# Start of a fused attention and feed-forward kernel: second k projection without filler before it, two normalizations in a row, other places for transposes and loads, last P V copied by two engines

## Chip, cores and metric

One core of one Trainium2 chip. The metric is the device time of one execution in microseconds (us), lower is better. The granted clock is 1.00 unless said otherwise. The kernel before takes 568.5 to 568.9 us (median of the runs beside each experiment); single executions range from 568.42 to 569.41.

## The reference

```python
# attention, batch 8, heads 8, seq 1024, head_dim 64; E and F (64 x 1024) shorten the sequence to 64
k_proj = einsum('ks,bhsd->bhkd', E, k);  v_proj = einsum('ks,bhsd->bhkd', F, v)
attn = softmax(q @ k_proj.T / sqrt(64));  attn_out = attn @ v_proj
# then a gated feed-forward block on 8192 tokens, d_model 512, d_ff 1536
g = x @ w_gate;  out = (g * sigmoid(g) * (x @ w_val)) @ w_out
```

## The kernel before

The program is a hand-made order of units. 16 chunks of 512 tokens (two per batch) go through the feed-forward block; TensorE's products of one chunk are mixed with the attention of later ones. Only the start, where batch 0 has to be worked through before the first product can run, is touched here. Names used below:

- `load_*`: DMAs issued from GpSimd, casting f32 to bf16. `load_w_gv(c0, c1, which)` loads columns 128*c0 to 128*c1 of the gate (0) and/or value (1) weights; block n is column range n, used by product f = n.
- `u_KV` k projection, `u_T` transposes of q, `u_S` scores and exp, `u_R` row sums and reciprocals (VectorE), `u_N` normalization (GpSimd), `u_A` transposes of the normalized scores, `u_PV*` times V and copy to xT.
- `turn` turns E or F by TensorE; `warm(n)` issues n matmuls on zeros whose result nobody reads.
- `put(s, ...)` puts a unit in slot s: slot 2t follows the gate product of step t, slot 2t+1 its value product.

```python
        u_S(0, 0, "g"); u_R(0, 0); u_N(0, 0)
        load_w_gv(1, 2, (1,))
        load_w_gv(2, 3)
        u_T(0, 2, "a", act)
        warm(2)
        u_KV(0, "k", (4, 8), at="y")
        turn(1, "a", (0,), dve)
        # ... KT0, T of u = 1 and 3, second turn of F: unchanged
        u_S(0, 2, "g"); u_R(0, 2); u_N(0, 2)
        load_w_gv(3, 5, (0,))
        u_S(0, 1, "g"); u_R(0, 1); u_N(0, 1)
        u_S(0, 3, "v"); u_R(0, 3); u_N(0, 3)
        load_w_gv(3, 5, (1,))
        # ... A of u = 0, 2; V projections; P V of the first token half
        f_mm(0, 0, 0, 0)
        u_A(0, 1, dve)
        f_mm(0, 0, 1, 0)
        u_PV2(0, 0, 0, 1, dve)
        u_A(0, 3, act)
        f_mm(0, 1, 0, 0)
        u_PV2(0, 0, 1, 1, act)
        f_mm(0, 1, 1, 0)
        # ...
        for i, u in enumerate(range(4, 8)):
            put(11 + i, u_T, 0, u)
```

(Calls on one line, and cuts, are marked by semicolons and "...".)

The softmax here doesn't subtract the row's maximum and nothing guards it: scores larger than these inputs give would overflow.

Of the kernel before, what the change touches and what calls it, by code (L numbers as in the profile page):

```python
# [34 lines left out]
def kernel(  # L35
# [68 lines left out]
    def load_q(b, ch, js=(0, 4), hs=(0, H)):  # L104
        if js[0] == 0 and hs[0] == 0:
            qb[b, ch] = q_pool.tile([P, H, 4, D], BF16, name="qb", tag="qb")
        js, hs = slice(*js), slice(*hs)
        nc.gpsimd.dma_start(  # L108
            out=qb[b, ch][:, hs, js, :].rearrange("p h j d -> p h (j d)"),
            in_=q[b, hs].rearrange("h (p c j) d -> p c h j d", c=2, j=4)[:, ch, :, js, :].rearrange(  # L110
                "p h j d -> p h (j d)"
            ),
        )

    def load_w_gv(c0, c1, which=(0, 1)):
        cs = slice(c0 * P, c1 * P)
        for wsrc, wdst in [((moe_w_gate, wg), (moe_w_val, wv))[i] for i in which]:
            nc.gpsimd.dma_start(
                out=wdst[:, :, cs],
                in_=wsrc[:, cs].rearrange("(t p) c -> p t c", p=P),  # L120
            )
# [11 lines left out]
    def bank(where, shape, dt, name):  # L133
        pool, tag = banks[where]
        return pool.tile(shape, dt, name=name, tag=tag)

    def copy(eng, out, in_):
        (nc.scalar.copy if eng is nc.scalar else eng.tensor_copy)(out=out, in_=in_)  # L138
# [107 lines left out]
    def u_T(b, u, at="a", eng=nc.scalar):  # L246
        ch, w = divmod(u, 4)
        g, i = divmod(w, 2)
        ps = bank(at, [P, 4, P], BF16, "qTp")
        src = qb[b, ch]  # L250
        for n in range(4):
            nc.tensor.transpose(  # L252
                out=ps[:, n, :],
                in_=src[:, 4 * g + n, 2 * i : 2 * i + 2, :].rearrange("p j d -> p (j d)"),
                identity=ident_bf[:],
            )
        t = aw.tile([P, 4, P], BF16, name="qT", tag="qT", bufs=4)
        copy(eng, t[:], ps[:])
        qT[b, u] = t
# [17 lines left out]
    def u_S(b, u, at="a"):  # L277
        ch, w = divmod(u, 4)
        g, i = divmod(w, 2)
        ps = bank(at, [P, 4, P], FP32, "sc")  # L280
        if (b, ch) in BY_DMA:
            t = qT[b, ch, "d"][:].rearrange("p (h i) t -> p i h t", i=2)[:, i, 4 * g : 4 * g + 4]
        else:
            t = qT.pop((b, u))
        for n in range(4):
            nc.tensor.matmul(  # L286
                out=ps[:, n, :], lhsT=t[:, n, :], rhs=BD[b % 2][:, 4 * g + n, :], start=True, stop=True
            )
        e = aw.tile([P, 4, 2, KP], FP32, name="ee", tag="ee", bufs=4)
        nc.scalar.activation(  # L290
            out=e[:].rearrange("p h j k -> p (h j k)"),
            in_=ps[:].rearrange("p a k -> p (a k)"),
            func=AF.Exp,
            scale=scale,
        )
        ee[b, u] = e

    def u_R(b, u):
        e = ee[b, u]
        z = aw.tile([P, 4, 2], FP32, name="zz", tag="zz", bufs=3)  # L300
        nc.vector.reduce_sum(out=z[:], in_=e[:], axis=AX.X)  # L301
        r = aw.tile([P, 4, 2], FP32, name="rr", tag="rr", bufs=4)
        nc.vector.reciprocal(out=r[:], in_=z[:])  # L303
        rr[b, u] = r

    def u_N(b, u, eng=nc.gpsimd):
        ch, w = divmod(u, 4)
        g, i = divmod(w, 2)
        if (b, ch) in BY_DMA:
            if (b, ch, "d") not in AA:  # L310
                AA[b, ch, "d"] = aw.tile([P, 4, H, KP], BF16, name="AAd", tag="AAd")
            a = AA[b, ch, "d"][:, 2 * i : 2 * i + 2, 4 * g : 4 * g + 4, :]
        else:
            a = AA[b, u] = aw.tile([P, 2, 4, KP], BF16, name="AA", tag="AA", bufs=4)
            a = a[:]
        eng.tensor_tensor(  # L316
            out=a.rearrange("p j h k -> p h j k"),
            in0=ee.pop((b, u))[:],
            in1=rr.pop((b, u))[:].unsqueeze(3).to_broadcast([P, 4, 2, KP]),
            op=ALU.mult,  # L320
        )

    def u_A(b, u, eng=nc.vector):
        ch, w = divmod(u, 4)
        g, i = divmod(w, 2)
        if (b, ch) not in AT:
            AT[b, ch] = aw.tile([P, 4, NPAIR, P], BF16, name="AT", tag="AT")
        ps = ps_a.tile([P, 2, 2, P], BF16, name="aTp", tag="pa")
        a = AA.pop((b, u))
        for pr in range(2):  # L330
            for j in range(2):
                nc.tensor.transpose(  # L332
                    out=ps[:, j, pr, :],
                    in_=a[:, j, 2 * pr : 2 * pr + 2, :].rearrange("p h k -> p (h k)"),
                    identity=ident_bf[:],
                )
        copy(eng, AT[b, ch][:, 2 * i : 2 * i + 2, 2 * g : 2 * g + 2, :], ps[:])
# [14 lines left out]
    def u_PV2(b, ch, g, i, eng):  # L352

        if (b, ch) not in xT:
            xT[b, ch] = x_pool.tile([P, NPAIR, CW], BF16, name="xT", tag=f"xT{ch}")
        ps = ps_a.tile([P, 2, CW // 2], FP32, name="pv", tag="pa")
        for n in range(2):
            nc.tensor.matmul(  # L358
                out=ps[:, n].rearrange("p (j t) -> p j t", t=P),
                lhsT=BDV[b % 2][:, 2 * g + n, :],  # L360
                rhs=AT[b, ch][:, 2 * i : 2 * i + 2, 2 * g + n, :],
                start=True,
                stop=True,
            )
        copy(eng, xT[b, ch][:, 2 * g : 2 * g + 2, 256 * i : 256 * (i + 1)], ps[:])

    def u_PV1(b, ch, pr, i, eng):

        ps = ps_a.tile([P, CW // 2], FP32, name="pv", tag="pa")
        nc.tensor.matmul(  # L370
            out=ps[:].rearrange("p (j t) -> p j t", t=P),
            lhsT=BDV[b % 2][:, pr, :],
            rhs=AT[b, ch][:, 2 * i : 2 * i + 2, pr, :],
            start=True,
            stop=True,
        )
        copy(eng, xT[b, ch][:, pr, 256 * i : 256 * (i + 1)], ps[:])
# [82 lines left out]
    def put(s, fn, *a):  # L460
        slots[s].append((fn, a))
# [34 lines left out]
    with tc.manual_schedule():  # L496
# [31 lines left out]
        def warm(n):  # L528

            ps = bank("v", [P, CW], FP32, "warm")  # L530
            for _ in range(n):
                nc.tensor.matmul(  # L532
                    out=ps[:], lhsT=zeros[:, 0:P], rhs=zeros[:],
                    start=True, stop=True,
                )


        dve, act = nc.vector, nc.scalar
# [20 lines left out]
        u_R(0, 0)  # L559
        u_N(0, 0)  # L560
        load_w_gv(1, 2, (1,))
        load_w_gv(2, 3)
        u_T(0, 2, "a", act)
        warm(2)
        u_KV(0, "k", (4, 8), at="y")
        turn(1, "a", (0,), dve)
        u_KT0((2, 4), "vg", (dve, dve, act, act))
# [3 lines left out]
        u_S(0, 2, "g")  # L571
        u_R(0, 2)
        u_N(0, 2)
        load_w_gv(3, 5, (0,))
        u_S(0, 1, "g")
        u_R(0, 1)
        u_N(0, 1)
        u_S(0, 3, "v")
        u_R(0, 3)
        u_N(0, 3)  # L580
        load_w_gv(3, 5, (1,))
        u_A(0, 0, act)
        u_V0w(0, 2, "y")
        u_V0(2, 3, "v")
# [1 line left out]
        u_A(0, 2, dve)  # L586
        u_V0(3, 4, "y")
        u_PV1(0, 0, 2, 0, dve)
        u_PV1(0, 0, 3, 0, act)
        f_mm(0, 0, 0, 0)  # L590
        u_A(0, 1, dve)
        f_mm(0, 0, 1, 0)
        u_PV2(0, 0, 0, 1, dve)
        u_A(0, 3, act)
        f_mm(0, 1, 0, 0)
        u_PV2(0, 0, 1, 1, act)
        f_mm(0, 1, 1, 0)
        nc.vector.memset(ks[1][64:P], 0.0)
        nc.vector.memset(BD[1][:], 0.0)
        nc.vector.memset(BDV[1][:], 0.0)  # L600
        load_w_gv(5, 7)
        load_q(0, 1, hs=(0, 4))
        load_q(0, 1, hs=(4, 8))
        load_w_gv(7, 9)
        load_w_gv(9, 11)
        load_w_gv(11, 12)
        load_q(1, 0)
        load_k(1)
        load_wo(0)
        load_wo(1)  # L610

        for i, u in enumerate(range(4, 8)):
            put(11 + i, u_T, 0, u)
            put(13 + i, u_S, 0, u)
            put(14 + i, u_R, 0, u)
            put(14 + i, u_N, 0, u)
            put((17, 18, 20, 21)[i], u_A, 0, u, nc.scalar)
# [26 lines left out]
        for t in range(NIT):  # L644
            c, f = divmod(t, NFT)
            i = 1 if t < 2 else None
# [39 lines left out]
```

## Time and profile before

| | kernel before |
|---|---|
| time, median of 3 | 568.7 us (568.54 to 569.03) |
| span of the profiled execution | 566.8 us |
| TensorE idle, 10 to 30 us | 1.6 us |
| TensorE idle, 30 to 50 us | 0.1 us |

The span is the time between the first and the last instruction. TensorE is busy for 99% of it, so only what makes TensorE start or stop earlier counts.

Two quantities are used all through. The **landing** of a load is its issue time plus its time to landing. The **lead** of a kernel at some instruction is how much earlier it starts there than the kernel before; I matched TensorE's weight loads of two traces from the end backwards, since the order is the same after the start.

### The profile page before, as it was taken

To read this page: it belongs to the slowest core of one execution; us is meant where nothing else is said; L and a number is where in the kernel's file an instruction comes from. 1 tells how busy PE (TensorE), PEld (TensorE's weight loads), DVE (VectorE), ACT (ScalarE), POOL (GpSimd) and SP (SyncE) were. 2 spreads that over 40 slices of the span, in tenths; PEclk is the share of its full clock that TensorE was granted. 3 is DMA by queue.
4 is the path that set the end of the run, shared out by engine and by line. 5 is a ranking of instruction groups with operands and counts; after the bars stand their busy time and mean duration, and the time that the engine had idled before them with its cause. 6 is when DMAs were issued, how large, how long until landed. Compare 5 with 4: busy or idle time off the path is not lost.

```text
span 566.8 us, 7925 instructions
## 1 busy us (share of the span) xinstructions
PE 560.3 (99%) x2960; PEld 266.2 (47%) x2960; DVE 339.2 (60%) x578; ACT 235.7 (42%) x416; POOL 113.0 (20%) x127
## 2 busy tenths in 40 slices
PE   8999999999999999999999999999999999999997
PEld 4654444444444444444444444444444444444444
DVE  3786664766476645766466655666547665545550
ACT  3564352444435443443434434354343543443222
POOL 6951250123012400123002230023100220000000
PEclk9999999999999999999999999999999999999999
DMA  9999979729913795029930399105990214100012
GB/s 206 191 198 189 176 130 201 134 57 189 194 46 74 117 199 113 38 57 168 189 72 37 77 184 205 38 20 104 196 183 19 58 37 75 38 37 31 26 39 93
DMA packets 112215, 62.78 MB, mean 111 GB/s; under 512 B 66352, under 2 KB 103472, under 8 KB 112176
## 3 DMA queue, kind: packets, MB, share of 16 engines
q0 software_dynamic: 43952, 29.49, 36.5%
q1 hardware_dynamic: 67392, 31.46, 25.6%
q10 hardware_dynamic: 832, 1.31, 0.7%
q8 instruction: 23, 0.38, 0.3%
q14 instruction: 16, 0.13, 0.1%
HBM read 60.29 MB, written 16.78 MB: 136 GB/s over the span
## 4 chain that ended last, share of the span: by engine, by line
PE 97%; ACT 1%; DMA 1%; DVE 0%; issue 0%; POOL 0%
PE yps L433 29%; PE vps L395 29%; PE gps L395 29%; PE kvp L150 3%; PE sc L286 2%; PE pv L343 2%; DMA Eraw<-in_E_dram 1%; ACT ee L290 0%; PE qTp L252 0%; PE aTp L332 0%; PE warm L532 0%; PE efp L520 0%; PE pv L358 0%; ACT AT L138 0%; POOL AA L316 0%
## 5 line engine op out<-in xcount | busy, mean ns | idle before, releaser
L414 DVE SCALAR_TENSOR_TENSOR s<-th,gps 128x512 f32<-128x512 f32 x191 | 129.7, 679 | 134.6 <-ACT th L407 134.3
L395 PE MATMUL vps<-xT,wv 128*128 128x512 bf16 (+1 forms) x776 | 197.5, 377 | 0.0
L395 PE MATMUL gps<-xT,wg 128*128 128x512 bf16 (+1 forms) x772 | 196.9, 377 | 0.0
L433 PE MATMUL yps<-wo,hT 128*128 128x512 bf16 (+1 forms) x780 | 194.5, 376 | 0.0
L407 ACT ACTIVATE th<-gps 128x512 f32<-128x512 f32 x191 | 114.0, 597 | 158.2 <-PE gps L395 151.8
L419 DVE TENSOR_TENSOR hT<-s,vps 128x512 bf16<-128x512 f32 x192 | 131.9, 687 | 20.8 <-DVE s L414 0.5
L316 POOL TENSOR_TENSOR AAd<-ee,rr 128x512 bf16<-128x512 f32 x56 | 58.4, 1042 | 342.0 <-issue 221.9
L433 PEld LDWEIGHTS <-hT 128*128 128x128 bf16 x780 | 76.1, 98 | 89.9
L395 PEld LDWEIGHTS <-wv 128*128 128x128 bf16 x776 | 73.9, 98 | 83.5 <-issue 3.2
L395 PEld LDWEIGHTS <-wg 128*128 128x128 bf16 x776 | 74.0, 98 | 80.9 <-issue 0.8
L443 ACT ACTIVATE ysb<-yps 128x512 f32<-128x512 f32 (+1 forms) x65 | 38.4, 591 | 77.7 <-PE yps L433 77.7
L138 ACT CAST xT<-pv 128x512 bf16<-128x512 f32 (+1 forms) x62 | 35.9, 582 | 51.3 <-PE pv L343 50.3
L301 DVE TENSOR_REDUCE zz<-ee 128x8 f32<-128x512 f32 x64 | 43.5, 679 | 21.9 <-ACT ee L290 21.9
L290 ACT ACTIVATE ee<-sc 128x512 f32<-128x512 f32 x64 | 37.9, 595 | 19.4 <-PE sc L286 18.2
L286 PEld LDWEIGHTS <-qTd 128*128 128x128 bf16 x224 | 17.2, 98 | 13.2
L343 PE MATMUL pv<-AT,BDV 128*128 128x512 bf16 x60 | 22.4, 379 | 0.0
L286 PE MATMUL sc<-BD,qTd 128*128 128x128 bf16 x224 | 21.6, 219 | 0.0
L303 DVE RECIPROCAL rr<-zz 128x8 f32<-128x8 f32 x64 | 13.0, 203 | 6.8 <-DVE zz L301 0.5
L108 POOL DMA_DIRECT2D qb<-in_q_dram x18 | 16.3, 906 | 1.4 <-POOLq L670 0.8
L150 PE MATMUL kvp<-kb,ET 128*64 128x512 bf16 (+1 forms) x72 | 15.5, 358 | 0.0
L162 DVE CAST BDV<-kvp 64x256 bf16<-64x256 f32 x7 | 3.0, 426 | 20.0 <-ACT ks L158 17.8
L150 PE MATMUL kvp<-vb,FT 128*64 128x512 bf16 x56 | 13.4, 382 | 0.0
(73 smaller groups left out, 140.8 us busy)
## 6 DMA issues: line engine op xcount, KB each, us to landing
out_dram<-ysb SPq DMA_DIRECT2D x63, 256.0 KB, 2.3
qb<-in_q_dram POOLq DMA_DIRECT2D x14, 512.0 KB, 17.7
kb<-in_k_dram POOLq DMA_DIRECT2D x7, 1024.0 KB, 11.0
vb<-in_v_dram POOLq DMA_DIRECT2D x7, 1024.0 KB, 13.6
wo<-in_moe_w_out_dram POOLq DMA_DIRECT2D x2, 768.0 KB, 20.6
kraw<-in_k_dram ACTq DMA_DIRECT2D x2, 512.0 KB, 4.8
qb<-in_q_dram POOLq DMA_DIRECT2D x4, 256.0 KB, 7.2
wg<-in_moe_w_gate_dram POOLq DMA_DIRECT2D x4, 256.0 KB, 7.3
```

Of the source, the lines that this page charges most:

```text
L138: (nc.scalar.copy if eng is nc.scalar else eng.tensor_copy)(out=out, in_=in_)
L150: nc.tensor.matmul(out=t[lo : lo + 64, h0:h1].rearrange("p h d -> p (h d)"), lhsT=w[:, j, :], rhs=src[b][:, h0:h1, j, :], start=(j == 0), ...
L286: nc.tensor.matmul(out=ps[:, n, :], lhsT=t[:, n, :], rhs=BD[b % 2][:, 4 * g + n, :], start=True, stop=True)
L290: nc.scalar.activation(out=e[:].rearrange("p h j k -> p (h j k)"), in_=ps[:].rearrange("p a k -> p (a k)"), func=AF.Exp, scale=scale,)
L301: nc.vector.reduce_sum(out=z[:], in_=e[:], axis=AX.X)
L316: eng.tensor_tensor(out=a.rearrange("p j h k -> p h j k"), in0=ee.pop((b, u))[:], in1=rr.pop((b, u))[:].unsqueeze(3).to_broadcast([P, 4, 2 ...
L395: nc.tensor.matmul(out=ps[:, ts], lhsT=(wg, wv)[w][:, kt, f * P : (f + 1) * P], rhs=x[:, kt, ts], start=(kt == 0), stop=(kt == NKT - 1),)
L407: nc.scalar.activation(out=th[:], in_=ps[:], func=AF.Tanh, scale=0.5)
L414: nc.vector.scalar_tensor_tensor(out=s1[:], in0=th[:], scalar=1.0, in1=g[:], op0=ALU.add, op1=ALU.mult)
L419: nc.vector.tensor_tensor(out=hT[c][:, f, :], in0=s1[:], in1=ps[:], op=ALU.mult)
L433: nc.tensor.matmul(out=yy[c][:, cs], lhsT=hT[c][:, f, i * P : (i + 1) * P], rhs=wo[:, f, cs], start=(f == 0), stop=(f == NFT - 1),)
L443: nc.scalar.activation(out=ysb[:, cs], in_=yy[c][:, cs], func=AF.Copy, scale=0.5)
```

## The change

The intent: take TensorE's waits out of the start. The second k projection no longer stands behind two filler matmuls; the normalizations u=2 and u=1 follow each other on GpSimd, with weight issues moved behind them; a transpose moves into a wait; the last P V is split so that VectorE and ScalarE copy half each. On the queue, block 7 is loaded ahead of the second chunk of q, and the transposes of that chunk move one product later.

```diff
--- before.py
+++ after.py
@@ -559,9 +559,8 @@
         u_R(0, 0)
         u_N(0, 0)
         load_w_gv(1, 2, (1,))
-        load_w_gv(2, 3)
+        load_w_gv(2, 3, (0,))
         u_T(0, 2, "a", act)
-        warm(2)
         u_KV(0, "k", (4, 8), at="y")
         turn(1, "a", (0,), dve)
         u_KT0((2, 4), "vg", (dve, dve, act, act))
@@ -571,14 +570,14 @@
         u_S(0, 2, "g")
         u_R(0, 2)
         u_N(0, 2)
-        load_w_gv(3, 5, (0,))
         u_S(0, 1, "g")
         u_R(0, 1)
         u_N(0, 1)
+        load_w_gv(2, 3, (1,))
         u_S(0, 3, "v")
         u_R(0, 3)
         u_N(0, 3)
-        load_w_gv(3, 5, (1,))
+        load_w_gv(3, 5)
         u_A(0, 0, act)
         u_V0w(0, 2, "y")
         u_V0(2, 3, "v")
@@ -586,31 +585,32 @@
         u_A(0, 2, dve)
         u_V0(3, 4, "y")
         u_PV1(0, 0, 2, 0, dve)
+        u_A(0, 1, dve)
         u_PV1(0, 0, 3, 0, act)
         f_mm(0, 0, 0, 0)
-        u_A(0, 1, dve)
+        u_PV2(0, 0, 0, 1, dve)
         f_mm(0, 0, 1, 0)
-        u_PV2(0, 0, 0, 1, dve)
         u_A(0, 3, act)
         f_mm(0, 1, 0, 0)
-        u_PV2(0, 0, 1, 1, act)
+        u_PV1(0, 0, 2, 1, dve)
+        u_PV1(0, 0, 3, 1, act)
         f_mm(0, 1, 1, 0)
         nc.vector.memset(ks[1][64:P], 0.0)
         nc.vector.memset(BD[1][:], 0.0)
         nc.vector.memset(BDV[1][:], 0.0)
         load_w_gv(5, 7)
+        load_w_gv(7, 8)
         load_q(0, 1, hs=(0, 4))
         load_q(0, 1, hs=(4, 8))
-        load_w_gv(7, 9)
-        load_w_gv(9, 11)
-        load_w_gv(11, 12)
+        load_w_gv(8, 10)
+        load_w_gv(10, 12)
         load_q(1, 0)
         load_k(1)
         load_wo(0)
         load_wo(1)
 
         for i, u in enumerate(range(4, 8)):
-            put(11 + i, u_T, 0, u)
+            put((12, 12, 13, 14)[i], u_T, 0, u)
             put(13 + i, u_S, 0, u)
             put(14 + i, u_R, 0, u)
             put(14 + i, u_N, 0, u)
```

## The prediction

> **What bounds the kernel now.** I read the page first: shares, chain, slices.
>
> ```profile
> PE 560.3 (99%) x2960; PEld 266.2 (47%) x2960; DVE 339.2 (60%) x578; ACT 235.7 (42%) x416; POOL 113.0 (20%) x127
> PE 97%; ACT 1%; DMA 1%; DVE 0%; issue 0%; POOL 0%
> PEclk9999999999999999999999999999999999999999
> ```
>
> TensorE is the whole bound, at full clock. The change touches only the first batch's first chunk, so the question is how much idle is there to be had. The second view, busy time by stretch, answers it.
>
> ```profile
> core 0: us, PE busy (x) PEld busy (x) DVE busy (x) ACT busy (x) POOL busy (x), PEclk, DMA share, GB/s
> 10.00:20.00 10.00, 8.76 (x111) 6.28 (x111) 6.48 (x18) 6.72 (x18) 7.27 (x9) 1.00 1.47 195
> 20.00:30.00 10.00, 9.64 (x65) 5.83 (x64) 7.37 (x13) 4.16 (x7) 8.83 (x13) 1.00 1.50 191
> 30.00:40.00 10.00, 9.99 (x73) 5.44 (x71) 8.11 (x15) 7.12 (x13) 5.34 (x6) 1.00 1.50 196
> ```
>
> Idle TensorE between 10 and 30 us is 1.24 + 0.36 = 1.6 us. Matmul ends are modelled and overlap, so that undercounts a little: matmuls stretched over a wait (x4 taking 0.89 us where the same four take 0.60 elsewhere) hide some more. From 30 us there is nothing. So the ceiling is about 2 us of 568.7, or 0.35%, and a 2% gain is impossible. What is left is to say how much of 2 us comes.
>
> The third view is the timeline, all engines, 11 to 25 us.
>
> ```profile
> 11.51 0.59 PE L532 MATMUL warm<-zeros 128*128 128x512 bf16 x2
> 12.04 1.06 PE L150 MATMUL kvp<-kb,ET 128*64 128x256 bf16 x8
> 13.02 0.33 PEld L520 LDWEIGHTS <-Fraw 64*128 64x128 bf16 x4 [0.20 <-DMA Fraw<-in_F_dram]
> 13.50 0.29 DVE L138 COPY FT<-efp 128x256 bf16<-128x256 bf16 x1 [0.46 <-PE efp L520]
> 13.82 0.61 DVE L138 CAST BD<-kTp 64x128 bf16<-64x128 f32 x2
> 14.46 0.75 DVE L138 COPY qT<-qTp 128x512 bf16<-128x512 bf16 x2
> ...
> 19.20 0.89 PE L395 MATMUL gps<-xT,wg 128*128 128x256 bf16 x4
> 20.83 0.38 PE L358 MATMUL pv<-AT,BDV 128*128 128x256 bf16 x2
> 22.11 0.38 PE L358 MATMUL pv<-AT,BDV 128*128 128x256 bf16 x2 [0.24 <-ACT AT L138]
> 22.52 0.59 ACT L138 CAST xT<-pv 128x512 bf16<-128x512 f32 x1 [0.47 <-PE pv L358]
> 22.76 0.78 PE L395 MATMUL gps<-xT,wg 128*128 128x256 bf16 x4
> ```
>
> The two warm-up matmuls are filler, yet the first F turn after them waits for F, and a row of VectorE work hangs on that turn. Later TensorE waits for a copy three times.
>
> The fourth view is each load by itself, from its issue to its landing (issue time plus time to landing):
>
> ```profile
> L118 POOL DMA_DIRECT2D wg<-in_moe_w_gate_dram x1: 745/745/745, 11.1 to 11.1; - x1
> DMA to landing us min/median/max: 10.0/10.0/10.0
> ```
>
> That is the second gate block (f=1): landed at 21.1 to 21.2, used at 21.27. By the same reading F lands at 5.0 + 7.9 = 12.9 (used 13.03), the last v piece at 18.0 (used 18.28), first gate block 18.7 (19.20), first value block 19.5 (20.16), second value block 21.5 (22.33), third blocks 22.2 and 22.9 (24.69 and 25.74), blocks 3-4 24.3 and 25.6 (26.6 and 27.46). The start-up rides just behind a saturated queue.
>
> **What the Trainium skill says.** "DMA: Bandwidth & Descriptors", section "SWDGE vs HWDGE vs iDMA": a load that casts must be issued from GpSimd. All these weights are cast from f32 to bf16, so they share one queue, and here they land in issue order. The same page, "Why small descriptors are slow (HBM only)": each packet carries a fixed overhead, 27% at 256 B. The trace agrees in direction: consecutive 128-column blocks (256 B) land 0.74 us apart for 128 KB, 173 KB/us, two-block loads 1.34 us apart for 256 KB, 191 KB/us. "VectorE: DVE Perf Modes", section "The TRN2 errata": a copy out of PSUM costs a fixed 120 (VectorE) or 172 (ScalarE) cycles plus one per element. At 0.96 and 1.2 GHz that gives 0.66/0.57 us for 512 and 0.39/0.36 us for 256 elements; the trace has 0.69/0.59 and 0.42/0.37. "TensorE: Matmul & The Clock Gate", section "What's actually happening": the clock drops only after about 3.4 us idle. Removing two warm-ups leaves no such gap, and every stretch has clock 1.00.
>
> **The change, part by part.**
>
> (1) Two warm-ups go: two starts 0.22 us apart, so the second k projection starts 0.43 us earlier, near 11.6. Its k half landed at 2.3 + 8.5 = 10.8, so it may. But the F turn behind it stays at 13.0, because F lands at 12.9 and TensorE is in order. VectorE then copies FT (13.50), two BD pieces, two qT, unchanged to 15.2, so the second and third scores stay. Only ScalarE gains: the k transposes come 0.2 us earlier (13.55 to 13.35), so its second FT copy and three exponentials move up by 0.15 to 0.2. Of 0.43 us, about 0.2 survives.
>
> (2) 0.2 us earlier at the first P V: 17.68 to 17.5. The V piece needing the last v load (18.28) cannot start before 18.05. So up to 0.2 survives here as well.
>
> (3) Normalizations u=2 and u=1 in a row on GpSimd. One takes 1.04 us, one weight issue 0.80. Before: u=2 ends 17.77, one issue, u=1 ends 19.55, u=3 at 20.55. After: 17.6, 18.6, then one issue, u=3 at 20.35. So u=1 is ready 0.9 us earlier, u=3 0.2.
>
> (4) Its transpose moves ahead of the last first-half P V (about 18.7 instead of 19.94), into a wait for ScalarE, and its VectorE copy (0.42) beside the first product. This removes the stop before P V (20.83: matmul issue stretched 0.24 us) and 0.22 us of TensorE work from the later path.
>
> (5) The last P V: one ScalarE copy of 512 (0.59) becomes copies of 256 on VectorE and ScalarE side by side (0.42, 0.37). The product at 22.76, stretched 0.78 against 0.60, loses its 0.18 us wait.
>
> Laid end to end on TensorE (f half product 0.44, transposes 0.22, P V 0.22): first gate product 19.04, held by xT copies to 19.77; P V 19.8; first value product 20.03 to 20.47; last transposes 20.48 to 20.70 after u=3 (20.35), copied by 21.49. The second gate block, issued at 11.13 as before behind the same bytes, lands at 21.16: the product runs 21.2 to 21.65, about 0.5 us waiting. P V 21.65 to 21.87, second value product to 22.31. Then the second token half. Before, that began effectively at 22.76 + 0.18 = 22.94. **Gain: 22.94 - 22.31 = 0.6 us**, one sum for parts 1 to 5, not to be added. The later stop near 25.6 (third value product waiting for VectorE) shifts with it.
>
> (6) The queue. Third value block: issued at 18.6 instead of 15.7, but its turn in the queue is only at 22.2, landing still 22.9. Blocks 3-4: gate issued near 20.4 instead of 17.7, its turn at 23.0; still ahead. Block 7 (256 KB, 1.4 us) goes before q's second chunk: its halves land at 31.0 and 32.4 instead of 29.6 and 31.0. The turns that read them move one product later, (with the gain) 32.0 and 33.5, so no wait. TensorE work is moved, not added: zero.
>
> Sum: 568.7 - 0.6 = **568.1 us**.
>
> **Rivals.** A: *transfers eat it.* F, last v, and the second gate block each leave 0.1 to 0.3 us. If that block lands 0.3 late, or all stops there, the gain is 0 to 0.3: 568.4 to 568.7. For: slack of 0.1 us at 21.27. Against: the stops after 21.27 (0.24 + 0.18) are copies, not loads. B: *late issues or q starve TensorE:* a wait near 26 or 33 us, 568.7 to 569.5. For: the queue's lead at the blocks 3-4 gate issue shrinks to about 2.6 us, q's slack to about 1. Against: loads then issued 3.8 us ahead of their turn never left the queue dry. C: *all idle goes*, because the block lands earlier or further bubbles (one of 0.29 us at 39.8, waiting for GpSimd) close: 567.5.
>
> **Range and chances.** Main path 0.6 with 0.5 probability, A 0.25, B 0.1, C 0.15. Runs scatter from 568.54 to 569.03. Range 567.4 to 568.7. 2% is 11 us, over five times the idle there is: faster 0.005, same 0.99, slower 0.005.
>
> **What would show it.** Right: the k projection near 11.6 and F turn still at 13.0; value product 2 (25.74 before) near 25.1; a stop of about 0.5 us on the second gate block before 21.2; none at the last P V; the same lead at 60 us as at 30. Wrong: that stop absent with the product well before 21 (gain over 1 us), a weight or q wait after 25 us (B), or a lead that shrinks between 30 and 60 us.

## The result, and the profile after

568.81 us (568.50 to 569.28, 4 runs) against 568.87 us (4 runs): ratio 0.9999, interval 0.9982 to 1.0017. Here and below a ratio is the mean time of one kernel's fast runs over that of the other's of the same rounds, so not quite the ratio of the medians quoted. The predicted gain of 0.6 us did not come, and 568.81 lies outside my range.

The page of the changed kernel first: TensorE's row and the chain that ended last, by engine.

```profile
PE 557.1 (98%) x2904; PEld 266.0 (47%) x2958; DVE 339.6 (60%) x579; ACT 235.6 (42%) x416; POOL 113.1 (20%) x127
PE 88%; DMA 8%; POOL 2%; issue 1%; ACT 0%; DVE 0%; POOLq 0%
```

The busy time cannot be compared: this trace has 54 matmul records fewer than weight loads, so some are missing. But the chain tells: it was 97% TensorE and 1% DMA before, now DMA and GpSimd hold 10% of it. The chain view between 20 and 64 us shows which (start, duration, who):

```profile
22.08 0.71 POOL wg L118
22.79 7.24 DMA wv<-in_moe_w_val_dram
...
31.04 11.50 DMA qb<-in_q_dram
...
42.56 18.88 DMA qTd<-qb
...
61.49 0.40 PE sc L286 x4
```

For 40 us the start of the scores of batch 1 hangs on the load queue, back to a weight issue at 22.08 us. (The queue's depth plays in: a ninth load waits for the landing of one eight places earlier, here the issue at 30.31 for the landing at 30.03, in the kernel before 28.61 for 28.32.) The timeline of TensorE shows what came of the steps (start, duration, engine, line, what; in brackets the wait):

```profile
11.52 1.06 PE L150 MATMUL kvp<-kb,ET 128*64 128x256 bf16 x8
13.18 0.43 PE L520 MATMUL efp<-ident_bf,Fraw 64*128 64x64 bf16 x4 [0.60 <-DMA Fraw<-in_F_dram]
21.29 0.61 PE L395 MATMUL gps<-xT,wg 128*128 128x256 bf16 x4 [0.24 <-DMA wg<-in_moe_w_gate_dram]
22.39 0.60 PE L395 MATMUL gps<-xT,wg 128*128 128x256 bf16 x4
25.19 1.02 PE L395 MATMUL vps<-xT,wv 128*128 128x512 bf16 x4
32.88 0.62 PE L252 MATMUL qTp<-ident_bf,qb 128*128 128x128 bf16 x8 [0.62 <-DMA qb<-in_q_dram]
```

The third value product starts at 25.19, before at 25.74: **the 0.55 us had been won** by 25 us. Then the transposes of q's second chunk wait for q. The table of leads tells the same step by step, with the plain cause of each step:

| at (kernel before, us) | lead of the changed kernel | what happened |
|---|---|---|
| 12.03, second k projection | +0.51 | no filler before it |
| 13.55, k transposes | +0.01 | F turn waited for F |
| 23.16, gate product of the second half | +0.55 | copies and transposes moved |
| 32.87, second q transposes | -0.25 | wait for q's second chunk, 0.80 |
| 40.12, transposes of batch 0 | +0.15 | wait for GpSimd of the kernel before gone |
| 41.22 | -0.18 | instead a wait for a ScalarE copy |
| 61.00, scores of batch 1 | -0.50 | wait for the transposed q, 0.32 |
| end | -0.50 | |

That is the profiled execution (569.04 us). Of the other three, two took 568.50 and 568.57, one 569.28.

Why is q late? I had worked out landings at 31.0 and 32.4 us. The two loads of q's second chunk in the kernel before, then in the changed one:

```profile
L108 POOL DMA_DIRECT2D qb<-in_q_dram x2: 770/775/780, 22.8 to 23.5; - x2
DMA to landing us min/median/max: 6.8/7.1/7.4
```
```profile
L108 POOL DMA_DIRECT2D qb<-in_q_dram x2: 795/800/805, 25.0 to 25.7; - x2
DMA to landing us min/median/max: 7.8/8.2/8.5
```

So 29.6 and 31.0 before, 32.8 and 34.2 after: 3.2 us later, of which block 7 accounts for 1.4. The DMA view of 20 to 30 us, in slices of 0.25 us, has the rest. Before:

```profile
GB/s 170 175 179 174 182 179 189 196 194 202 197 187 199 199 197 195 201 189 188 174 190 197 174 180 188 195 197 189 193 199 199 201 199 184 195 197 203 203 191 188
```

After:

```profile
GB/s 183 169 174 183 175 179 181 138 70 32 92 109 160 174 186 180 182 180 197 178 152 141 115 111 109 145 180 184 186 170 174 188 180 166 161 144 170 174 168 181
```

A queue that never fell below 170 GB/s falls to 32 at 22 us and to 110 near 26 us. By the packet records it had moved 369 KB less by 30 us than in the kernel before (52 KB less already at 21 us, from a later start): about 1.7 us of its work. GpSimd's timeline shows what had changed for the queue:

```profile
16.72 2.04 POOL L316 TENSOR_TENSOR AA<-ee,rr 128x512 bf16<-128x512 f32 x2 [1.07 <-ACT ee L290]
18.71 0.81 POOL L118 DMA_DIRECT2D wv<-in_moe_w_val_dram  x1
19.54 1.06 POOL L316 TENSOR_TENSOR AA<-ee,rr 128x512 bf16<-128x512 f32 x1
20.53 0.80 POOL L118 DMA_DIRECT2D wg<-in_moe_w_gate_dram  x1
```

The third value block is issued at 18.71 (15.73 before) and the gate part of blocks 3 and 4 at 20.53 (17.72 before). And GpSimd sat idle for 1.07 us before the normalizations, waiting for exp: the value block's issue, 0.80 us, would have fitted there free.

### The profile page after: what moved, and what is told of

Its sections match the earlier page's. It is cut to its first block, busy times and chain, and to the rows that moved or that the text cites. A ratio compares the mean times of both kernels' runs of the same rounds, so it can differ in the third digit from the quotient of the medians.

```text
span 567.3 us, 7868 instructions
## 1 busy us (share of the span) xinstructions
PE 557.1 (98%) x2904; PEld 266.0 (47%) x2958; DVE 339.6 (60%) x579; ACT 235.6 (42%) x416; POOL 113.1 (20%) x127
## 4 chain that ended last, share of the span: by engine, by line
PE 88%; DMA 8%; POOL 2%; issue 1%; ACT 0%; DVE 0%; POOLq 0%
PE yps L433 28%; PE vps L395 27%; PE gps L395 26%; DMA qTd<-qb 3%; PE sc L286 2%; PE kvp L150 2%; PE pv L343 2%; DMA qb<-in_q_dram 2%; DMA Fraw<-in_F_dram 1%; DMA wv<-in_moe_w_val_dram 1%; POOL wv L118 0%; POOL AA L316 0%; POOL wg L118 0%; POOL qb L108 0%; PE efp L520 0%
## 5 line engine op out<-in xcount | busy, mean ns | idle before, releaser
L395 PE MATMUL gps<-xT,wg 128*128 128x512 bf16 (+1 forms) x750 | 194.1, 377 | 1.2 <-DMA wg<-in_moe_w_gate_dram 0.2
L433 PE MATMUL yps<-wo,hT 128*128 128x512 bf16 (+2 forms) x763 | 191.8, 376 | 0.7
```

The lines of the kernel that those rows point to most:

```text
L395: nc.tensor.matmul(out=ps[:, ts], lhsT=(wg, wv)[w][:, kt, f * P : (f + 1) * P], rhs=x[:, kt, ts], start=(kt == 0), stop=(kt == NKT - 1),)
L433: nc.tensor.matmul(out=yy[c][:, cs], lhsT=hT[c][:, f, i * P : (i + 1) * P], rhs=wo[:, f, cs], start=(f == 0), stop=(f == NFT - 1),)
```

## The experiments

Three theories. **D**: the later issues let the queue run dry, and that makes q late. **Q**: block 7 ahead of q makes it late, whatever the issues. **C**: the slow spell was chance. Each group ran on one chip with the kernel before beside it, five rounds.

### 1. The changed kernel again

> The changed kernel again, unaltered, to tell habit from chance. In its first profile the queue moved only 69 KB between 22 and 23 us (193 KB in the kernel before), packets of up to 0.65 us followed until 29 us, q's second chunk landed at 32.8 and 34.2 us, and TensorE waited 0.8 us for it at 32.9 us and 0.3 us for the transposed q near 61 us. Theory D (queue runs dry because the third value block and the gate blocks 3-4 are issued 3 us later): the dip at 22 to 23 us and q landing after 32.5 us come again in every profile. Theory C (the slow packets are chance): no dip, q lands at 31.0 and 32.4 as I had predicted, no wait at 32.9 us, and the lead of 0.55 us reaches the end (span 0.5 us under the kernel before).

568.75 us (568.53 to 569.95) beside 568.56 of the kernel before; ratio 1.0001 (0.9988 to 1.0015). The DMA view of 20 to 30 us:

```profile
GB/s 175 172 184 174 177 183 140 87 94 44 82 166 176 199 195 160 184 188 186 184 160 119 100 98 119 158 154 162 170 160 156 170 167 149 161 166 180 179 179 188
```

The same two dips. (The 69 and 193 KB of the expectation are 76 and 195 by the DMA view.) The lead was +0.78 at 25.7 us. Then TensorE lost 0.75 us to waits for gate and value blocks 5-6 (landed 29.5 and 30.8), the loads behind the second dip, and 1.1 us to the wait for q (33.6 and 35.0 us); the transposed q came at 62.35, and the lead at the end was -1.4 us. Waits for weights and for q after 25 us are what rival B of the prediction had named. C is out: the spell is the change's own; its depth varies.

### 2. Issues early again

```diff
-        load_w_gv(2, 3, (0,))
+        load_w_gv(2, 3)
...
         u_N(0, 1)
-        load_w_gv(2, 3, (1,))
+        load_w_gv(3, 5, (0,))
...
         u_N(0, 3)
-        load_w_gv(3, 5)
+        load_w_gv(3, 5, (1,))
```

> Changed kernel, but third value block issued with its gate block before the normalizations, and gate blocks 3-4 before the last one (each weight issue one place earlier; order of the normalizations as changed). Theory D: no dip at 22 us, slow packets gone, q's second chunk lands near 31.0 and 32.4 us, wait for q at most 0.2 us, transposed q before 60 us, span 0.3 to 0.6 us shorter than the changed kernel's. Theory Q (only block 7 ahead of q does the harm, whatever the issue times): q still 1.4 us later than in the kernel before (31.0) or later, wait for q stays at 0.5 us or more. Theory C: no systematic difference to the changed kernel.

568.50 us (567.77 to 568.71); ratio 0.9996 (0.9983 to 1.0008). No dip (190 to 193 KB in each us from 22 to 26), q at 31.3 and 32.7 with no wait for it, transposed q at 59.6 us. D's mechanism holds. But the trace had a new stop that no theory had: TensorE waited 0.7 us for the **first value block**, which landed at 20.75 instead of 19.5, and the lead at the end was nil.

### 3. q ahead of block 7, issues late

```diff
-        load_w_gv(7, 8)
         load_q(0, 1, hs=(0, 4))
         load_q(0, 1, hs=(4, 8))
+        load_w_gv(7, 8)
```

> Changed kernel, but block 7 (256 KB) is issued after q's second chunk rather than ahead of it. Theory D: the dip at 22 us stays; q lands 1.4 us earlier than in the changed kernel (31.4 and 32.8), so the wait at 32.9 us goes, but the transposed q still lands after 61 us and TensorE waits there, so the end gains little (0 to 0.3 us). Theory Q: wait at 32.9 us gone and the whole lead of 0.5 us reaches the end. Theory C: as Q when no slow spell falls in.

568.74 us (568.54 to 570.16); ratio 1.0009 (0.9996 to 1.0022). Dip as in the changed kernel (109 KB from 22 to 23 us). No wait for q any more (30.7 and 32.0), but the transposed q landed at 61.16 and TensorE waited for it: the lead fell from +0.14 to -0.21 there. So q's place decides where the lost transfer time shows, and cannot give it back. Again the first value block came late, 20.6.

### 4. Both mends

The diffs of 2 and 3 together, on the changed kernel.

> Both edits: early issues and q ahead of block 7, so that only the TensorE order, the normalizations' order, the dropped warm-ups and the split P V remain of the change. Theory D and theory Q both: no dip, no wait for q, transposed q before 60 us, the lead of 0.5 to 0.6 us at 25 us reaches the end: 568.2 us where the kernel before has 568.8. If the end still shows no gain, something between 33 and 61 us takes it back (the ScalarE copy wait near 41 us of 0.3 us).

567.97 us (567.78 to 568.49, five runs: three near 567.8 to 568.0, two near 568.45) beside 568.56; ratio 0.9990 (0.9978 to 1.0003). No dip, no wait for q, transposed q at 59.4. The profiled execution was again one with a late first value block (20.69, TensorE waits 0.8 us), span 566.7, and its lead at the end was 0.04 us. Two kinds of executions, 0.6 us apart: a second cause was still open.

**Theory F.** The traces have, besides the loads, single packets of 16 KB on an instruction queue, 0.95 us long, each on one of the 16 DMA engines. The first of them starts near 19 us. I take it that a load lands when its share on every engine has, so that such a packet holds up whatever load that engine is on. The packet records fit: in the kernel before, the loads ahead of blocks 3-4 ran at some 180 GB/s until 21.5 us, and a rest of them trickled on at 11 to 15 GB/s, about a sixteenth, from 22.0 to 22.5. The records do not name the engine. The packet's start fell at 18.5 to 18.7 us in the three kernels with a late first value block, and at 18.9 to 19.1 in the three without (there the next load, the second gate block, lands 1.5 to 1.7 us after the one before it, where 0.74 is usual).

### 5. The late issues alone

On the kernel before:

```diff
-        load_w_gv(2, 3)
+        load_w_gv(2, 3, (0,))
...
         u_N(0, 2)
-        load_w_gv(3, 5, (0,))
...
         u_N(0, 1)
+        load_w_gv(2, 3, (1,))
...
         u_N(0, 3)
-        load_w_gv(3, 5, (1,))
+        load_w_gv(3, 5)
```

> The kernel before with one part of the change alone: the third value block issued after the normalizations u=2 and u=1, gate blocks 3-4 after u=3. TensorE's order, block 7 and the turns stay as before. Theory D (late issues let the queue run dry): dip at 22 to 23 us (under 120 KB in that us, 190 before), slow packets near 25 us, q's second chunk about 1 us later than in the kernel before (29.6 and 31.0), transposed q after 60.5 us; the end 0 to 0.5 us later than in the kernel before. Rival (the dip needs TensorE's new order): no dip, landings as before within 0.2 us.

568.80 us (568.42 to 569.17) beside 568.56; ratio 1.0004 (0.9991 to 1.0016). The DMA view of 20 to 30 us:

```profile
GB/s 177 170 183 176 177 183 145 41 40 49 98 182 178 168 201 187 184 197 184 197 166 125 72 109 100 170 197 182 193 174 143 174 184 193 188 186 201 197 199 205
```

Both dips, with TensorE's order untouched: the late issues are enough. q landed at 30.7 and 32.0 (29.6 and 31.0), the transposed q at 60.82. TensorE took it up at 60.88 and its lead (0.19 from an earlier start) fell by 0.06 us there. The kernel before had 1.2 us to spare there; the dip takes most of that, so it hurts only a kernel that is ahead or a dip that is deeper.

### 6. The two warm-ups alone

```diff
         u_T(0, 2, "a", act)
-        warm(2)
         u_KV(0, "k", (4, 8), at="y")
```

> The kernel before without the two warm-up matmuls, nothing else. My prediction's part 1: k projection 0.4 us earlier, F turn held by F at 12.8 to 13.1, about 0.2 us left at the first P V, and without the other parts less than 0.2 us at 25 us, nothing measurable at the end. Theory F (TensorE's own instruction fetch, a 16 KB packet of 0.95 us on one DMA engine, delays whichever load that engine is on; when it starts before about 18.8 us it is the first value block): if the fetch starts before 18.8 us here, first value block lands at 20.6 instead of 19.5 and TensorE waits 0.5 us or more for it; if after, not.

568.93 us (568.42 to 569.00) beside 568.56; ratio 1.0002 (0.9989 to 1.0016). The k projection came 0.45 us earlier, the F turn 0.16. The instruction packet started at 18.76 and the first value block landed at 20.79. TensorE's timeline:

```profile
20.84 0.61 PE L395 MATMUL vps<-xT,wv 128*128 128x256 bf16 x4 [0.83 <-DMA wv<-in_moe_w_val_dram]
```

Lead -0.73 there, -0.47 at the end. So in this execution taking away filler whose result nobody reads *lost* 0.47 us.

### 7. Both mends, warm-ups put back

```diff
         u_T(0, 2, "a", act)
+        warm(2)
```

> The version with both mends (early issues, q ahead of block 7), with the two warm-ups put back. Theory F: instruction fetch starts after 18.8 us, first value block lands at 19.5 us, the 0.8 us wait for it is gone, second gate block at 21.1 takes the fetch instead, lead over the kernel before at 25 us 0.4 to 0.6 us, kept to the end: 568.0 in every run rather than 567.8 and 568.4 by turns. Rival (the first value block comes late because of the earlier k projection or the issue order, not the fetch): with the k projection late again the block still lands after 20.5 in this order of issues, or comes in time although the fetch starts before 18.8.

567.94 us (567.88 to 568.03, 4 runs) beside 568.56; ratio 0.9988 (0.9974 to 1.0001). Packet at 19.14, first value block at 19.52, no wait for it; 0.3 us for the second gate block (21.33); lead +0.47 at the second half's gate product, +0.50 at the end. All runs within 0.15 us: the second kind of execution (two of five in experiment 4) did not come in these four, nor in the five of experiment 12, which has the warm-ups too.

### 8. Fewer warm-up instructions by float32

The first 15 warm-ups became 7 float32 matmuls of 256 columns and one of the old kind.

> The version with both mends, with the first 15 warm-up matmuls replaced by 7 float32 ones and one of the old kind (same TensorE time, 8 pairs of instructions fewer), so that the instruction fetch comes 8 pairs later in the program. Theory F: fetch after 18.8 us, first value block at 19.5 us, no 0.8 us wait, lead at 25 us 0.5 to 0.6 us and kept, 567.9 us in most runs. Rival as above: first value block still after 20.5 us. If the fetch does not move, the experiment says nothing on F.

568.03 us (567.96 to 568.46, 4 runs); ratio 0.9991 (0.9977 to 1.0004). Inconclusive by its own terms: the trace shows 23 weight loads before 8 us as before, so each float32 matmul ran as two pairs and no instruction was saved. The packet stayed at 18.61 and the block late at 20.69.

### 9. Six more pairs of instructions, no more work

```diff
-        warm(11)
+        warm(10)
+        warm(7, 64)      # seven matmuls of 64 columns
```

in the kernel before; all of it is over before E arrives at 5.9 us.

> The kernel before with 6 more pairs of TensorE instructions and no more work: one of the first eleven warm-up matmuls (512 columns) becomes seven of 64, all of them before E arrives at 5.9 us. Nothing after that is touched. Theory F (TensorE's instruction fetch comes after a fixed number of its instructions and delays the load on its DMA engine): the fetch comes 6 pairs earlier in the program, before 18.8 us, the first value block lands at 20.6 us instead of 19.5, TensorE waits 0.7 us for it, and the end is 0.3 to 0.5 us later than the kernel before (568.9). Rival (late first value block has another cause): nothing changes, fetch or no fetch.

The packet moved from 19.12 to 18.38, the first value block from 19.47 to 20.52. TensorE's weight loads:

```profile
20.57 0.33 PEld L395 LDWEIGHTS <-wv 128*128 128x128 bf16 x4 [0.24 <-DMA wv<-in_moe_w_val_dram]
```

Lead -0.46 there, -0.19 at the end (a later wait for a copy gave some back), less than I had expected. More instructions of TensorE, all long done, moved the packet: so I take it for TensorE's instruction fetch. With it the block came late. This is one profile; the scatter of the packet in one kernel is 0.16 us (18.89 and 19.05 in the two of the changed kernel), the shift 0.74. The time, 569.39 (568.69 to 570.26) beside 568.54, ratio 1.0014 (1.0002 to 1.0026), probably overstates it: 570.26 was a run with the clock at 0.997 and 569.39 one at 0.999. Of the three at 1.000, two took 568.69 and 568.72, and one 569.44, which stays unexplained.

### 10. Five more warm-ups dropped

In the version with both mends:

```diff
         turn(0, "v")
-        warm(4)
...
-        warm(1)
         u_S(0, 0, "g")
```

> The version with both mends (no two warm-ups) and 5 more warm-up matmuls dropped, the four after E's turns and the one before the first scores, which stand in TensorE's idle time; so the fetch comes 5 pairs later in the program. Theory F: fetch after 18.8 us, first value block at 19.5 us, no wait of 0.8 us for it, lead at 25 us 0.5 to 0.7 us, kept to the end, 567.8 us in every run; as good as or 0.1 us better than the version with both mends and the two warm-ups. Rival: first value block after 20.5 us again. A third outcome: TensorE's clock drops for want of warm-ups, which the clock row would show.

569.20 us (567.85 to 571.37, 6 runs) beside 568.54; ratio 1.0013 (0.9997 to 1.0028). The third outcome: the clock fell. Busy time and clock of 5 to 25 us (clock is the third number from the end):

```profile
5.00:15.00 10.00, 7.58 (x47) 5.24 (x44) 3.68 (x10) 3.67 (x9) 5.98 (x8) 0.66 1.36 209
15.00:25.00 10.00, 9.35 (x121) 7.38 (x121) 7.07 (x18) 6.35 (x17) 9.11 (x12) 1.00 1.40 162
```

Cut finer, the clock was 1.00 from 4.7 to 8.1 us and 0.50 from 8.1 to 14.9. In those first 3.4 us TensorE was busy for 1.89, with no gap over 1.0 us. By 13 us the kernel was 1.5 us behind the kernel before. The packet came at 20.75 and the first value block at 19.43, in time, as F has it, but with everything later this is no clean test. The two runs with a clock of 1.00 took 567.85 and 568.42; F had 567.8 in every run, and neither was profiled.

### 11. Last P V on one engine again

```diff
-        u_PV1(0, 0, 2, 1, dve)
-        u_PV1(0, 0, 3, 1, act)
+        u_PV2(0, 0, 1, 1, act)
```

in the version of experiment 7.

> The version with both mends and the two warm-ups, but the last P V of the first chunk as before: one ScalarE copy of 512 columns in place of two of 256 on VectorE and ScalarE. My prediction's part 5: the product after it stretched by about 0.2 us again (its third slice waits for the copy), lead at 25 us 0.2 us smaller. Rival: the loss is given back by the VectorE wait at the third value product (0.19 us in both kernels), as VectorE starts its gate work earlier; then the lead at 26 us is the same within 0.05 us.

568.19 us (568.10 to 569.23) beside 568.54; ratio 1.0000 (0.9988 to 1.0012). The product after it, first in experiment 7, then here:

```profile
22.48 0.60 PE L395 MATMUL gps<-xT,wg 128*128 128x256 bf16 x4
22.91 0.60 PE L395 MATMUL vps<-xT,wv 128*128 128x256 bf16 x4
```
```profile
22.37 0.78 PE L395 MATMUL gps<-xT,wg 128*128 128x256 bf16 x4
22.98 0.49 PE L395 MATMUL vps<-xT,wv 128*128 128x256 bf16 x3
```

From one start to the next 0.43 us with the split, 0.61 without: the wait of 0.18 us is back. The lead at the end is 0.14 us smaller than in experiment 7, though the second gate block happened to land 0.14 earlier here. The rival's give-back did not come. All this is read from one trace each, taken on two chips. By its times, with two of five runs at 568.93 and 569.23, this version cannot be told from the kernel before.

### 12. Early issues and warm-ups, block 7 left ahead of q

The diffs of 2 and 7 on the changed kernel, without that of 3.

> The changed kernel with early issues and the two warm-ups put back, block 7 left ahead of q as in the change. If the dry queue alone makes q late (theory D), q's second chunk lands at 31.4 and 32.7 us, TensorE reaches its turns at 32.4 and 33.5 us without a wait over 0.1 us, and the whole lead of 0.5 us reaches the end: 567.9 to 568.0 us, as with both mends. If block 7 ahead of q costs by itself, TensorE waits 0.2 us or more there and the end is that much later. Theory F: instruction fetch after 18.8 us, first value block at 19.5 us.

**567.96 us** (567.86 to 568.06, 5 runs) beside 568.53 (568.47 to 569.41, 8 runs); ratio 0.9988 (0.9974 to 1.0002). The interval just reaches 1, but no run of one kernel overlaps any of the other's. Its DMA view of 20 to 30 us and its q transposes:

```profile
GB/s 180 169 182 180 169 185 180 186 199 200 198 198 185 195 197 203 197 191 189 199 201 201 195 172 168 164 184 199 186 182 183 174 178 183 180 196 196 197 199 193
```
```profile
32.07 0.61 PE L252 MATMUL qTp<-ident_bf,qb 128*128 128x128 bf16 x8
```

No dip, q at 31.3 and 32.7 (for the change itself I had predicted 31.0 and 32.4), no wait; packet at 18.94, first value block at 19.36. Lead +0.57 at the second half's gate product, +0.55 at the end. Block 7 ahead of q costs nothing when the queue does not run dry: Q is out.

### What ties the first value block to the packet

| kernel | packet starts | first value block lands |
|---|---|---|
| late by 1.0 to 1.3 us: b_tiny, a_qfirst, a_both_few, a_both, a_early, b_nowarm | 18.38, 18.54, 18.61, 18.62, 18.71, 18.76 | 20.52, 20.62, 20.69, 20.69, 20.75, 20.79 |
| in time: a_again, b_late, a_early_warm, after, before, a_both_warm, a_both_warm_pv, a_both_less | 18.89, 18.93, 18.94, 19.05, 19.12, 19.14, 19.16, 20.75 | 19.47, 19.26, 19.36, 19.58, 19.47, 19.52, 19.44, 19.43 |

All 14 profiles split at 18.8 us. The changed kernel, without the two warm-ups, has two profiles in the lower row, so the late block goes with the packet's time and not with the warm-ups as such.

## Why the prediction was wrong, point by point

- **Bound and ceiling**: right. TensorE is the bound, 2% out of reach, about 2 us to be had.
- **(1) Warm-ups**: k projection earlier (11.52, "near 11.6"), F turn held by F (13.18, "at 13.0"): right. The "about 0.2 us" that survives depends on when F lands: 0.01 in the changed kernel's profile, 0.32 in experiment 6. What the step did not have at all is that TensorE's progress sets when the 16 KB packet comes (experiment 9). Four instructions fewer, with a start some tenths earlier, can bring it to where the first value block comes late (18.76 in experiment 6).
- **(2) and (3)**: the 0.2 us of part 1 did not come through in the changed kernel's profile. The first P V starts at 17.67 (17.68 before), and the normalizations at 16.72 (16.73 before), when exp is done. Normalization u=1 ended 0.8 us earlier (18.76 instead of 19.60), near the 0.9 I had, u=3 at 20.59 as before and not 0.2 earlier. The sum did not suffer because the second gate block, which lands after all of this, hides it. That is luck as far as these parts go.
- **(4), (5)**: right in kind and size. The stop before P V at 20.83 is gone, the product after the last P V lost its 0.18 us wait (experiment 11 measured 0.18), and the second gate block stops TensorE instead (landed 21.24; I had 21.16). The sum for 25 us was 0.6, measured 0.55. The value product that I put "near 25.1" came at 25.19.
- **(6) The queue: the step that failed.** It said of the gate blocks 3-4 "issued near 20.4 instead of 17.7, its turn at 23.0; still ahead", and of q "its halves land at 31.0 and 32.4 ... so no wait". The issue time was right (20.53). But it was not "still ahead": the queue ran dry at 22 us, lost about 1.7 us of transfers by 30 us, and q landed at 32.8 and 34.2. The turn was misread. I took it for the landing of the load before (23.0), and by then the queue had long been at work on the next. Packet sizes show it: single blocks move in packets of 256 B, double ones such as blocks 3-4 in packets of 512 B. From 21.5 to 22 us, before and after the change:

```profile
DMA packets 265, 0.10 MB, mean 192 GB/s; under 512 B 141, under 2 KB 265, under 8 KB 265
DMA packets 322, 0.08 MB, mean 160 GB/s; under 512 B 322, under 2 KB 322, under 8 KB 322
```

The kernel before moves 124 packets of blocks 3-4 here (the first at 21.52 us by the packet records), the changed one none: its first starts at 22.08, 1.55 us after the issue at 20.53, when the small packets have all but run out (1.53 and 1.52 us in experiments 1 and 5), and the full rate is back at 23. So an issue at 20.4 was some 1.1 us ahead of need, less than these 1.5, and not 2.6; of the two late issues it is this one whose packets were missing. Rival B had named it, "a wait near 26 or 33 us", with a chance of only 0.1; the argument against it, that loads issued 3.8 us ahead never left the queue dry, counted from landings too and said nothing on a shorter lead.
- **"The same lead at 60 us as at 30"**: wrong for the same reason. I had looked at each load's slack for its own first use, and not at the far end of the queue: its last users (the transposed q at 61 us) had 1.2 us to spare, and every us of transfer lost at 22 comes out of that.
- The 0.66/0.57 and 0.39/0.36 us that I gave for copies are estimates from the cycles and clocks of the skill's VectorE page; my sums used the trace's durations.
- The range ended at 568.7, inside the scatter of the kernel before (up to 569.03 in its first three runs). It was too narrow at the top even had the chance of B been right.

Shown: late issues make the dips (5, and 2 against the changed kernel), the dips make q late and take the lead (1, 2, 3, 12), the 16 KB packet goes with a late first value block (the table; 9, where it was moved on purpose). That it is TensorE's instruction fetch, and that it delays the block by holding one engine, is argued from 9 and from the trickle of packets, not shown directly. Open: why there is a second dip near 26 us, where the loads had been issued some 4 us ahead, counted by landings (packets of 0.2 to 0.65 us stand there among those of 0.06), and where the faster executions of the changed kernel (568.50 to 568.58, four of nine) lose the gain, as the two profiled ones were among the slower.

## What to carry to other kernels

When a DMA queue is full from start to finish of a stage, an issue may move only as late as the queue's lead allows, whatever the first use of its data: look at the queue's GB/s row, at when the first packets of a load run (not at when the load before it lands), and at the last user down the line. An idle gap on the issuing engine is the place for an issue; the change moved one out of such a gap and gained nothing for the work it made room for. And in a start whose loads land just in time, a few tenths of a us and a few instructions shift where such a packet, by all appearance an instruction fetch, falls; what looks like two kinds of executions may be that (not shown: no fast execution of experiment 4 was profiled).

## What the Trainium skill lacked or had wrong

- "DMA: Bandwidth & Descriptors", section "Anatomy of one DMA — SWDGE (gpsimd) path", gives a fixed cost of about 2 us per DMA and puts most of it down to completion. For the late load of these runs 1.52 to 1.55 us passed between issue and first packet already (20.53 to 22.08), and the full rate came 2.5 us after the issue; the runs do not split this further.
- The skill has the fetch of instructions in blocks of 16 KB through a DMA queue and calls its cost "mostly hidden" ("Runtime: NRT & Kernel Launch", section "Instruction fetch mechanics"). It does not say that such a fetch can hold up a load: here the first value block landed 1.0 to 1.3 us late in the six profiles in which a 16 KB packet of 0.95 us began before 18.8 us.
- "TensorE: Matmul & The Clock Gate", section "What's actually happening": the clock drops after some 3.4 us idle. In experiment 10 it fell to 0.50 at 8.1 us, though TensorE had been busy for 1.89 of the 3.4 us before and no wait between matmuls was over 1.0 us there; the runs do not show which measure of activity decides. So my prediction's use of it, that only one long gap would matter, is too simple for such a start; the "only" is mine.
